# Seven block products for the second channel product, turns by DMA, and one written TensorE order

## The chip, the cores and the metric

The kernel runs on one core of a Trainium2 chip. The metric is the device time of one execution in microseconds, taken as the median of several runs. The profile is of one execution.

The engines go by short names: PE is TensorE (matmuls and transposes; PEld is its loading of weights), DVE is VectorE, ACT is ScalarE, POOL is GpSimd, SP is SyncE. SP and POOL issue the transfers (DMA). PSUM is the memory of eight banks per partition into which PE writes; each bank holds 512 fp32 numbers a partition.

## The reference

Four batches of windowed attention (8 heads, 768 positions, 64 numbers a head; a query sees the 4 first positions and the last 128) feed a token mixing and a channel mixing:

```python
def _attn_ref(q, k, v, n_sink, window):
    B, H, S, D = q.shape
    scores = (1.0 / np.sqrt(D)) * np.matmul(q, k.transpose(0, 1, 3, 2))
    pos = np.arange(S)
    rel = pos[:, None] - pos[None, :]
    keep = (pos[None, :] < int(n_sink)) | ((rel >= 0) & (rel < int(window)))
    scores = np.where(keep, scores, -1000000000.0)
    a = np.exp(scores - np.max(scores, axis=-1, keepdims=True))
    a = a / (np.sum(a, axis=-1, keepdims=True) + 1e-09)
    return np.matmul(a, v).astype(np.float32)

def _moe_ref(x, w_tok1, w_tok2, w_ch1, w_ch2):   # x: (4, 768, 512)
    xt = x.transpose(0, 2, 1)
    h = np.maximum(xt @ w_tok1, 0.0) @ w_tok2     # 768 -> 256 -> 768
    u = x + h.transpose(0, 2, 1)
    h2 = np.maximum(u @ w_ch1, 0.0) @ w_ch2       # 512 -> 1536 -> 512
    return (u + h2).astype(np.float32)
```

## The kernel before

**Pairs.** The 32 (batch, head) combinations are handled as 16 pairs of heads, pairs 0 to 3 for batch 0 and so on. For a pair, q and k are loaded with their rows on the partitions, turned to have head numbers on the partitions (`qT`, `kT`), multiplied to scores in three groups `g` of 256 keys, exponentiated on ACT, masked, and multiplied with v, which carries a column of ones for the row sums. The four sink positions have small products of their own (`score_sinks`, `sink_values`), with copies of their k columns (`kTs`) and v rows (`v_sink`, written by `sink_rows`).

**Loads and turns.** Pairs 0 to 3 are loaded by SP in fp32 and cast. From pair 4 on POOL issues loads that cast on the way (L106), which also bring v and the weights. `transposed(p)` (L461) turns q and k of a pair by 24 PE transposes into a score tile; DVE and ACT copy the result out in halves, and `cleared` (L482) zeroes the strip of the tile that the scores need to be zero. Batch 0 and pair 4 use `turn` instead.

**Token mixing.** Per batch and half `g` of the 512 channels, `mix_h` makes 12 matmuls of 256 columns (`x_sb` with `w_tok1`), and three `mix_u` make four each (`h1T` with `w_tok2`); DVE adds x to give `u_sb`. `turned_u` (L787) turns u by PE into `uT`.

**Channel mixing** (`mix_channels`, L903). `v1(ft, half)` multiplies `uT` with `w_ch1`, 4 matmuls of 384 columns, and a relu stores a block of `v1T`: 12 blocks `ft` of hidden numbers by 2 halves of the rows. Then `out_part` multiplies `v1T` with `w_ch2`: per tile of 128 rows 12 matmuls of 512 columns into one bank; DVE adds u (L938), SP stores 128 rows (L944). The very last row tile goes in three column blocks (L960).

**Score tiles.** PSUM is cut into two score tiles of two banks each (tag `sc`) and four single banks (tag `mx`). `scores` of groups 1 and 2 go by quarters (`by_quarters`): 16 small matmuls that skip what the window masks; the parts skipped must hold zeros, which is what `cleared` restores.

**Order.** A planner in the program (`Plan`, L250) simulates the engines with fixed costs and emits instructions in that order. An `Op` is an instruction for any engine, with its costs and what it depends on; a `unit` is a stretch of PE work, with its needs of banks and the ops that follow it. Three lists of units are merged: `first` (attention and token mixing of batch 0), `main` (channel mixing) and `side` (all later attention and token mixing). `MERGED` (L47) says for each side unit after how many main units it comes; units of `first` are put in wherever the simulation finds them ready. Each engine runs its instructions in program order.

Of the kernel before, what the change touches and what calls it, by code (L numbers as in the profile page):

```python
# [16 lines left out]
def kernel(  # L17
# [13 lines left out]
    nc = tc.nc  # L31
# [15 lines left out]
    MERGED = (  # L47
# [5 lines left out]
    )  # L53
    NQ = 6
    MASKED_BY_PE = [(p, g) for p in range(NHP) for g in range(NT // 2) if (p, g) != (NHP - 1, 0)]
# [4 lines left out]
    att_pool = ctx.enter_context(tc.tile_pool(name="att", bufs=2))  # L60
# [3 lines left out]
    osb_pool = ctx.enter_context(tc.tile_pool(name="osb", bufs=3))  # L64

    psum = ctx.enter_context(tc.tile_pool(name="psum", bufs=1, space=bass.MemoryType.PSUM))
    TAGS = {"sc": 2, "mx": 4}

    given = {}

    sc = [psum.tile([P, 2, 2, 4, D], FP32, name=f"ps_sc{n}", tag=f"sc{n}", bufs=1) for n in range(TAGS["sc"])]

    def bank(tag, *shape, dtype=FP32, slot=None):

        n = given[tag].pop(0) if slot is None else slot
        if tag == "sc":
            return sc[n]
        return psum.tile([P, *shape], dtype, name=f"ps_{tag}", tag=f"{tag}{n}", bufs=1)
# [5 lines left out]
    def rows_of(pidx, n):  # L84

        b, hp = pairs[pidx]
        return (q, k)[n][b, 2 * hp:2 * hp + 2].rearrange("h (p j) d -> p h j d", j=NT)
# [67 lines left out]
    keep_warm(7, 0)  # L155
# [27 lines left out]
    NKB = 2  # L183
# [28 lines left out]
    x_sb = [singles.tile([P, NT, DM], BF16, name=f"x_sb{b}") for b in range(B)]  # L212
# [37 lines left out]
    class Plan:  # L250
        def __init__(self):
            self.free = {"PE": 0.0, "ACT": 0.0, "DVE": 0.0, "SP": 0.0, "POOL": 0.0}
            self.queue, self.landings = 0.0, []
            self.half = False
            self.pending = []
            self.held = {t: [()] * n for t, n in TAGS.items()}

# [9 lines left out]
        def slots(self, tag):  # L267

            free = []
            for n, readers in enumerate(self.held[tag]):  # L270
                if all(r.done is not None for r in readers):
                    free.append((max((r.done for r in readers), default=0.0), n))
            return sorted(free)

        def spare(self):
            return self.slots("mx")[0][1]

        def start_pe(self, op):
            t = self.ready(op)
            if t is None:  # L280
                return None
            for tag, banks in op.need.items():
                free = self.slots(tag)
                if len(free) < len(banks):
                    return None
                t = max(t, free[len(banks) - 1][0])
            return max(t, self.free["PE"])
# [23 lines left out]
        def commit_pe(self, op, t):  # L311
            for tag, banks in op.need.items():
                given[tag] = [n for _, n in self.slots(tag)[:len(banks)]]
                for n, readers in zip(given[tag], banks):
                    self.held[tag][n] = readers
# [6 lines left out]
        def run(self, first, main, side):  # L322

            first, main = [list(u) for u in first], list(main)
            order = [[int(n) for n in unit.split("/")] for unit in MERGED.split()]
            side, behind = [side[n] for n, _ in order], [n for _, n in order]
            placed = 0
            while any(first) or main or side or self.pending:
                o = self.other()
                tm = self.start_pe(main[0]) if main else None  # L330
                ts = self.start_pe(side[0]) if side else None
                pick = "side" if side and (not main or behind[0] <= placed) else "main"
                t = tm if pick == "main" else ts
                early = [(t, u) for u in first if u for t in [self.start_pe(u[0])] if t is not None]
                if early:
                    soonest = min([t for t, _ in early] + ([] if t is None else [t]))
                    stay = [(t, u) for t, u in early if self.half and u[0].half and t <= soonest + SWITCH]
                    te, u = next((e for e in stay + early if e[0] <= soonest + (SWITCH if e in stay else 40.0)), (None, None))
                    if u is not None and (o is None or o[0] > te):
                        self.commit_pe(u.pop(0), te)  # L340
                        continue
# [11 lines left out]
                if pick == "main":  # L353
                    placed += 1
                else:
                    behind.pop(0)
                self.commit_pe((main if pick == "main" else side).pop(0), t)
# [35 lines left out]

    QH = NT // 2

    def prepare(p):
# [21 lines left out]
        free = ([("sk", p - 2)] if p >= 2 else [], [("s", p - NKB)] if p >= NKB else [])  # L418
# [10 lines left out]
        tiles["kT", p] = kT  # L429
# [31 lines left out]
    def transposed(p):  # L461

        def run():
            ps = turned_bank(p)
            for n in range(2):
                for j in range(NT):
                    for x in range(2):
                        rows = ds(D * x, D)
                        in_order(nc.tensor.transpose(ps[:, x, n, j], bfs[p, n][rows, j], ident[rows, rows]))  # L469
                tiles["ps_" + "qk"[n], p] = [ps[:, x, n].rearrange("d j p -> d p j") for x in range(2)]  # L470

        then = [*done["qT", p], *done["kT", p], done["kTs", p]]
        then.append(cleared(p, then))
        return piece(
            350, run, [done["q_bf", p], done["k_bf", p]], {"sc": [then]}, then, [("tq", p), ("tk", p)],
        )

    def turned_bank(key):

        tiles["ps_turned", key] = bank("sc")  # L480
        t = tiles["ps_turned", key].bitcast(BF16).rearrange("d x n b c -> d x n (b c)")[:, :, :, 2 * D:8 * D]
        return t.rearrange("d x n (j p) -> d x n j p", j=NT)  # L482

    def cleared(key, readers):

        op = Op(
            {"DVE": 400.0}, lambda e: in_order(nc.vector.memset(tiles["ps_turned", key][0:D, :, :, 3], 0.0)), readers,
        )
        op.urgent = 2
        return op  # L490
# [22 lines left out]
    def scores(p, g):  # L513
# [28 lines left out]
        def run():  # L542
            if ("pT", p) not in tiles:
                tiles["pT", p] = pt_pool.tile([P, 2, NT, 2, P], BF16, name="pT")
# [7 lines left out]
        def exp(e):  # L552
            in_order(nc.scalar.activation(  # L553
# [4 lines left out]
        def mask(e):  # L558
            pt = part(tiles["pT", p][:, :, ds(2 * g, 2)])
# [549 lines left out]
```

## Time and profile before

| | |
|---|---|
| runs | 207.47, 207.51, 207.58 us, median 207.51 us |
| span of the profiled execution | 206.7 us |
| PE busy | 199.5 us (97%) |
| DVE, ACT, POOL busy | 114.8, 119.0, 67.3 us |
| TensorE clock granted | full speed in all slices |
| data moved | 21.58 MB by DMA, in 73,223 packets |
| last matmul ends | 203.8 us |

A line of a group gives source line, engine, operation, output and input, their shapes and count, then busy time, the mean duration of one in ns, and the idle time of the engine just before it. In a list in order of time a line has start, length, engine, source line, operation and count. A matmul's length is from its start to the modelled end of its pipeline, so lengths of neighbours overlap, and the distance between starts is what a matmul costs. A line of the chain names engine, tile and source line, and its share of the span.

### The profile page before, as it was taken

What the parts mean: (1) busy time and instruction counts of PE and PEld (TensorE: products, weight loads), DVE (VectorE), ACT (ScalarE), POOL (GpSimd) and SP (SyncE); (2) the same over time, 40 slices, a digit from 0 to 9 for tenths busy, and PEclk for the clock granted to TensorE, in tenths of its full rate; (3) what the DMA queues carried; (4) which work ended last, traced back from release to release, by engine and by line L of the source; (5) the groups of instructions that cost most, each with busy time, mean ns of one, the idle gap of its engine ahead of it and who ended that gap; (6) DMA issues with size and microseconds to landing.
All of it is one profiled execution on the core that took longest, in us unless ns stands there. A gap on an engine that the chain in (4) does not pass through costs nothing.

```text
span 206.7 us, 5560 instructions
## 1 busy us (share of the span) xinstructions
PE 199.5 (97%) x2377; PEld 119.8 (58%) x2377; DVE 114.8 (56%) x263; ACT 119.0 (58%) x225; POOL 67.3 (33%) x86
## 2 busy tenths in 40 slices
PE   6798999999999999999999999999999999999994
PEld 2344795565565665666665555656655555565443
DVE  4687545649767777566675775784357252000222
ACT  4599666878744744888676443977562105773000
POOL 6099687696499984441000000000000000000000
PEclk9999999999999999999999999999999999999999
DMA  6999999999999999596001121100001212000223
GB/s 197 293 228 137 165 190 176 170 160 197 175 184 175 186 190 182 79 107 43 0 3 54 51 101 55 54 0 3 0 3 51 101 54 101 0 3 0 101 101 102
DMA packets 73223, 21.58 MB, mean 104 GB/s; under 512 B 63216, under 2 KB 70256, under 8 KB 73200
## 3 DMA queue, kind: packets, MB, share of 16 engines
q0 software_dynamic: 67232, 11.80, 72.7%
q1 hardware_dynamic: 5968, 9.45, 12.8%
q8 instruction: 18, 0.29, 0.6%
q14 instruction: 5, 0.04, 0.1%
HBM read 26.75 MB, written 6.29 MB: 160 GB/s over the span
## 4 chain that ended last, share of the span: by engine, by line
PE 86%; DMA 7%; DVE 2%; POOL 1%; ACT 1%; issue 0%; SPq 0%; POOLq 0%
PE ps_mx L121 78%; PE ps_sc L121 4%; DMA w_tok<-in_moe_w_tok_dram 4%; DMA v_sink_f<-in_v_dram 3%; PE ps_sc L469 2%; PE ps_mx L439 1%; POOL v_aug L114 1%; PE ps_mx L124 1%; SPq L200 0%; DVE u_sb L765 0%; POOL v_sink L130 0%; DVE qT L130 0%; PE ps_mx L451 0%; DVE kT L130 0%; DVE x_sb L664 0%
## 5 line engine op out<-in xcount | busy, mean ns | idle before, releaser
L121 PE MATMUL ps_mx<-w_ch,v1T 128*128 128x512 bf16 (+2 forms) x312 | 67.5, 363 | 0.0
L121 PE MATMUL ps_mx<-uT,w_ch 128*128 128x384 bf16 x384 | 66.3, 326 | 0.3 <-DVE recip L661 0.3
L553 ACT ACTIVATE pT<-ps_sc 128x1024 bf16<-128x1024 f32 (+1 forms) x48 | 44.5, 955 | 12.1 <-PE ps_sc L121 11.8
L121 PEld LDWEIGHTS <-w_ch 128*128 128x128 bf16 x384 | 36.2, 98 | 24.5 <-issue 1.5
L134 ACT ACTIVATE v1T<-ps_mx 128x384 bf16<-128x384 f32 x74 | 36.1, 493 | 16.5 <-PE ps_mx L121 16.0
L121 PEld LDWEIGHTS <-v1T 128*128 128x128 bf16 x312 | 28.2, 98 | 26.9 <-issue 0.7
L938 DVE TENSOR_TENSOR o_sb<-ps_mx,u_sb 128x512 f32<-128x512 f32 x23 | 15.9, 690 | 37.2 <-PE ps_mx L121 37.2
L121 PEld LDWEIGHTS <-w_tok 128*128 128x128 bf16 x192 | 18.4, 98 | 7.0 <-DMA w_tok<-in_moe_w_tok_dram 1.2
L106 POOL DMA_DIRECT2D q_bf<-in_q_dram x24 | 19.7, 824 | 4.6 <-DMA w_ch<-in_moe_w_ch_dram 2.0
L106 POOL DMA_DIRECT2D k_bf<-in_k_dram x24 | 19.6, 822 | 4.5 <-DMA w_ch<-in_moe_w_ch_dram 2.2
L114 POOL DMA_DIRECT2D v_aug<-in_v_dram x16 | 16.5, 1030 | 10.6 <-PE ps_mx L121 5.6
L765 DVE TENSOR_TENSOR u_sb<-ps_mx,x_sb 128x512 bf16<-128x512 f32 x20 | 13.2, 687 | 9.0 <-PE ps_mx L121 8.9
L136 DVE TENSOR_SCALAR v1T<-ps_mx 128x384 bf16<-128x384 f32 x22 | 12.2, 558 | 7.8 <-PE ps_mx L121 7.0
L121 PE MATMUL ps_mx<-v_aug,pT 128*128 128x65 bf16 x352 | 15.5, 194 | 0.0
L121 PEld LDWEIGHTS <-pT 128*128 128x128 bf16 x352 | 13.8, 97 | 2.7 <-issue 0.6
L121 PE MATMUL ps_sc<-qT,kT 64*64 64x192 bf16 (+3 forms) x288 | 15.0, 252 | 0.0
L561 DVE TENSOR_TENSOR pT<-pT,mask_main 128x1024 bf16<-128x1024 bf16 (+1 forms) x24 | 13.9, 618 | 0.0
L121 PE MATMUL ps_mx<-h1T,w_tok 128*128 128x256 bf16 x96 | 13.4, 272 | 0.0
L121 PE MATMUL ps_mx<-x_sb,w_tok 128*128 128x256 bf16 x96 | 12.0, 273 | 0.9 <-DMA w_tok<-in_moe_w_tok_dram 0.9
L130 DVE COPY qT<-ps_sc 128x384 bf16<-128x384 bf16 x11 | 6.1, 558 | 11.8 <-ACT qT L128 11.8
L664 DVE TENSOR_TENSOR x_sb<-ps_mx,recip 128x384 bf16<-128x384 f32 x22 | 11.6, 549 | 0.1
L128 ACT ACTIVATE kT<-ps_sc 128x384 bf16<-128x384 bf16 x16 | 7.3, 489 | 6.9 <-DVE qT L130 6.9
(74 smaller groups left out, 166.3 us busy)
## 6 DMA issues: line engine op xcount, KB each, us to landing
out_dram<-o_sb SPq DMA_DIRECT2D x23, 256.0 KB, 2.0
v_aug<-in_v_dram POOLq DMA_DIRECT2D x16, 192.0 KB, 7.0
w_ch<-in_moe_w_ch_dram POOLq DMA_DIRECT2D x8, 384.0 KB, 8.9
q_bf<-in_q_dram POOLq DMA_DIRECT2D x24, 96.0 KB, 7.0
k_bf<-in_k_dram POOLq DMA_DIRECT2D x24, 96.0 KB, 6.0
q_f<-in_q_dram SPq DMA_DIRECT2D x4, 384.0 KB, 5.9
k_f<-in_k_dram SPq DMA_DIRECT2D x4, 384.0 KB, 6.2
w_tok<-in_moe_w_tok_dram POOLq DMA_DIRECT2D x2, 384.0 KB, 8.5
```

Of the source, the lines that this page charges most:

```text
L106: in_order(nc.gpsimd.dma_start(out=out[:, h], in_=rows[:, h]))
L114: in_order(nc.gpsimd.dma_start(out=v_aug.rearrange("p i t d -> p (i t) d")[:, :, 0:D], in_=v[b].rearrange("h s d -> (h s) d")[2 * hp * S:2 ...
L121: in_order(nc.tensor.matmul(*args, skip_group_check=True, **kwargs))
L128: in_order(nc.scalar.activation(out, in_, AF.Copy))
L130: in_order({"DVE": nc.vector, "POOL": nc.gpsimd}[e].tensor_copy(out=out, in_=in_))
L134: in_order(nc.scalar.activation(out, in_, AF.Relu))
L136: in_order(nc.vector.tensor_scalar_max(out=out, in0=in_, scalar1=0.0))
L553: in_order(nc.scalar.activation(part(tiles["pT", p][:, :, ds(2 * g, 2)]), of_keys(tiles["ps_s", p, g])[:, :, 0:width(g)], AF.Exp, scale=scale,
L561: in_order(nc.vector.tensor_tensor(out=pt, in0=pt, in1=m, op=ALU.mult))
L664: in_order(nc.vector.tensor_tensor(out=x_sb[b][:, :, ds((2 * hp + i) * D, D)], in0=tiles["ps_o", p, i][:, :, 0:D], in1=tiles["recip", p, i ...
L765: in_order(nc.vector.tensor_tensor(out=u_part(b, g, s0, n), in0=tiles["ps_u", b, g, s0], in1=x_sb[b][:, s0:s0 + n, c0:c0 + cn], op=ALU.add,))
L938: in_order(nc.vector.tensor_tensor(out=o_sb.rearrange("p (g c) -> p g c", g=2), in1=u_rows(b, st), in0=tiles["ps_out", b, st].rearrange("p ...
```

## The change

1. **Seven products.** For batches 1 to 3 the second channel product is cut into 2 by 2 blocks (row halves by hidden halves, hidden halves by column halves) and made from seven block products in place of eight, by a scheme with four sums of v1 blocks (`add_up`: S1 to S4, S3 written over a v1 block) and four differences of weight blocks (`weight_sums`: T1 to T4, made once). Each product covers 384 rows by 256 columns and is made in two parts, `x` (two row tiles sharing a bank) and `y` (one row tile). Banks `a` and `c` go on accumulating after DVE has read them, and DVE adds each state to the output blocks: seven evictions in a part. An `x` part is 14 units of 6 matmuls, a `y` part 7 units of 6.
2. **Turns by DMA.** q and k of pairs 8 to 15 are turned by 16 DMA transposes, and u of batches 2 and 3 by 12, one after each `mix_u`; all are issued by SP. `turned_u` and `transposed` remain for what comes earlier. The q, k loads of these pairs take rows in another arrangement.
3. **One order.** `ORDERED` lists every PE unit by stream and number: `s m t o h g` are the first attention and token mixing, `a` the later attention, `k` the later token mixing, `c` the first channel product (24 units a batch), `x` and `y` the second (`x0` to `x23` are batch 0, undivided).
4. **Banks.** `choose` may give banks of the second score tile to other uses once the first streams are done; scores go by quarters only on the first score tile; `transposed` takes two plain banks; `cleared` goes.
5. **Smaller moves.** Sink rows go by two small DMAs of SP for each pair and no longer by ACT; masks of key groups 1 and 2 may go to POOL as four selects; `att` and `kT` buffers go from 2 to 3; `x_sb` from 4 to 2; stores are of a whole part (512 KB for `x`, 256 KB for `y`).

```diff
-    MERGED = (
-        "1/0 0/2 2/4 3/9 4/15 5/16 6/16 7/19 8/23 9/24 10/26 11/27 12/28 15/30 14/30 13/31 16/32 17/32 18/33 "
...
+    ORDERED = (
+        "t0-1 m0 s0 m1 s1 t2-3 m2-3 s2-3 o0 m4 s4 t4 m5 s5 t5 o1 m6-7 o2 s6 t6 o3 s7 o4 m8 t7 s8-9 g0 m9 s10-11 "
+        "g1 o5-6 m10 a0 s12 o7 g2 o8 g3-4 h0-1 g5 a1 h2-4 g6 h5-6 a2 c0-3 a3 h7 g7 c4-7 a4 c8 a5 c9-12 a6-7 "
+        "c13-15 a8 c16 a9-10 c17-21 a11 k0 x0-2 a12 k1 c22-23 a13 k2-3 x3-6 a14 x7 a15 x8-10 a16 x11 a17-18 "
+        "x12-14 k4 x15-16 k5-7 x17-19 a19 x20-23 c24 a20-22 c25-27 a23 c28-30 a24 c31-33 a25-26 c34 a27 c35-36 k8 "
+        "c37-39 a28-30 c40 x24 a31 c41-43 k9 c44 k10 a32-33 x25 k11 a34 c45-47 x26 k12 x27-28 a35 x29-31 k13 x32 "
+        "k14 a36-37 x33 y0 a38 y1-2 x34-35 y3 k15 y4 a39 y5 x36 c48 y6 c49 a40 x37 a41-42 c50-54 a43 c55-56 k16 "
+        "c57-60 a44-45 c61-64 a46 c65 a47 x38 c66-67 x39 c68 a48 c69 a49 k17-18 c70 k19 c71 k20 x40-41 k21-22 "
+        "x42-44 y7-8 x45-46 k23 y9 x47 y10-11 x48 y12 x49 c72-73 y13 x50-51 c74-87 x52 c88-91 x53 c92-95 x54 y14 "
+        "x55-56 y15 x57-58 y16 x59-61 y17 x62-63 y18-19 x64-65 y20"
     )
+    ORDER = (1, 2, 7, 6, 4, 5, 3)
...
+    BY_SEVEN = range(1, B)
+    BY_DMA = 2 * NHP
...
+        if pidx >= BY_DMA:
+            return rows.rearrange("h (j p) d -> p h j d", p=P)
...
+        if p >= BY_DMA:
+            def turn(e, n):
+                if not n:
+                    tiles["qT", p] = att_pool.tile([P, S], BF16, name="qT2")
+                in_order(nc.sync.dma_start_transpose(
+                    out=(kT if n else tiles["qT", p]).rearrange("c (t p) -> c t p", t=NT),
+                    in_=bfs[p, n].rearrange("p t h d -> p (t h d)"),
+                ))
...
-            (by_quarters if quarters else by_halves)(tiles["ps_s", p, g])
+            (by_quarters if quarters and tiles["ps_s", p, g] is sc[0] else by_halves)(tiles["ps_s", p, g])
...
         def mask(e):
+            if e == "POOL":
+                for n in range(2):
+                    nk = 2 if n == 0 or g < NT // 2 - 1 else 1
+                    for i in range(2):
+                        pt = tiles["pT", p][:, i, 2 * g:2 * g + nk, n]
+                        in_order(nc.gpsimd.affine_select(
+                            out=pt, in_=pt, compare_op=ALU.is_ge, fill=0.0, base=-n,
+                            pattern=[[0, nk], [1 - 2 * n, P]], channel_multiplier=2 * n - 1,
+                        ))
+                return
...
-                copy(e, v_sinks[p % NHP][r:r + n_sink, i], vs[p][0:n_sink, i, 0])
+                in_order(nc.sync.dma_start(out=v_sinks[p % NHP][r:r + n_sink, i], in_=vs[p][0:n_sink, i, 0]))
...
+            def turn(e):
+                in_order(nc.sync.dma_start_transpose(
+                    out=tiles["mix", b][2].rearrange("c (g t p) -> c g t p", g=2, p=P)[:, g, 2 * s0:2 * (s0 + n)],
+                    in_=u_part(b, g, s0, n).rearrange("p t c -> p (t c)"),
+                ))
...
+            s1 = op("S1", lambda: part(0), a21, a22, ALU.add, v[1, 0] + v[1, 1] + before)
+            s3 = op("S3", a21, a11, a21, ALU.subtract, v[0, 0] + [s1])
+            s2 = op("S2", lambda: part(1), lambda: part(0), a11, ALU.subtract, v[0, 0] + [s1])
+            s4 = op("S4", lambda: part(2), a12, lambda: part(1), ALU.subtract, v[0, 1] + [s2])
...
+        TERMS = {
+            1: ((0, 0), "B11"), 2: ((0, 1), "B21"), 3: ("S4", "B22"), 4: ((1, 1), "T4"),
+            5: ("S1", "T1"), 6: ("S2", "T2"), 7: ("S3", "T3"),
+        }
...
+            a1 = evict("a1", (0, 0), lambda: u_block(0, 0))
+            a6 = evict("a6", (1, 0), lambda: u_block(1, 0))
+            c7 = evict("c7", (1, 1), lambda: u_block(1, 1))
+            a5 = evict("a5", (1, 1), lambda: sb(1, 1), [c7])
+            a3 = evict("a3", (0, 1), lambda: u_block(0, 1))
+            c4 = evict("c4", (1, 0), lambda: sb(1, 0), [a6])
+            b2 = evict("b2", (0, 0), lambda: sb(0, 0), [a1])
...
+                        for t in range(n):
+                            for k in range(c * KC, (c + 1) * KC):
+                                mm(
+                                    ps[:, t], left(a_name, k, t0 + t), right(b_name, k),
+                                    start=(before is None and t == 0 and k == 0), stop=(k == NH - 1),
+                                )
...
+        x, y = products(0, 2), products(2, 1)
+        x, y = [u for m in ORDER for u in x[m]], [u for m in ORDER for u in y[m]]
+        done["out", b] = [x[-1], y[-1]]
...
+        for name, out, in0, in1, of in (
+            ("T1", t1, b12, lambda: b11, ()), ("T2", t2, b22, t1, ("T1",)),
+            ("T3", t3, b22, lambda: b12, ()), ("T4", t4, b21, t2, ("T2",)),
+        ):
```

More of the change, by code (lines that the diff above doesn't have):

```diff
@@ L320, in commit_pe, with run @@
             self.pending.extend(op.then)
[L322 to L328, printed above, removed]
-                o = self.other()
[L330 to L341, printed above, removed]
+        def run(self, units, early):
+            early = len(early)
+            units = list(units)
+            while units or self.pending:
+                self.late = early == 0
+                o = self.other()
+                t = self.start_pe(units[0][1]) if units else None
                 if o is not None and (t is None or o[0] <= t):
@@ L392, in piece, with joined, run @@
         return op
+    def joined(*units):
+        def run():
+            for u in units:
+                u.fn()
+        need = {}
+        for u in units:
+            for f in u.then:
+                f.deps = [d for d in f.deps if d is not u]
+            for tag, banks in u.need.items():
+                need.setdefault(tag, []).extend(banks)
+        return unit(
+            sum(u.size for u in units), run, [d for u in units for d in u.deps], need,
+            [t for u in units for t in u.then], half=units[0].half,
+        )
     QH = NT // 2
@@ L468, in run @@
                         rows = ds(D * x, D)
[L469 to L473, printed above, removed]
+                        in_order(nc.tensor.transpose(ps[x][:, n, j], bfs[p, n][rows, j], ident[rows, rows]))
+                tiles["ps_" + "qk"[n], p] = [ps[x][:, n].rearrange("d j p -> d p j") for x in range(2)]
+        readers = [[done["qT", p][x], done["kT", p][x]] for x in range(2)]
+        readers[0].append(done["kTs", p])
         return piece(
-            350, run, [done["q_bf", p], done["k_bf", p]], {"sc": [then]}, then, [("tq", p), ("tk", p)],
-        )
[L478 to L490, printed above, removed]
+            350, run, [done["q_bf", p], done["k_bf", p]], {"mx": readers}, [op for r in readers for op in r],
+            [("tq", p), ("tk", p)],
+        )
     def width(g):
```

425 lines of the change are left out of this document (278 added, 147 removed), and 4 rows, old and new, of the table MERGED.

## The prediction

> **What bounds the kernel now.** First the page's head, the clock row and the chain of waits; then the busy time by stretch of time; then TensorE's (PE's) instructions in order of time; last the groups and the DMA issues.
>
> ```profile
> span 206.7 us, 5560 instructions
> PE 199.5 (97%) x2377; PEld 119.8 (58%) x2377; DVE 114.8 (56%) x263; ACT 119.0 (58%) x225; POOL 67.3 (33%) x86
> PEclk9999999999999999999999999999999999999999
> PE 86%; DMA 7%; DVE 2%; POOL 1%; ACT 1%; issue 0%; SPq 0%; POOLq 0%
> ```
>
> The span is 206.7 us; the runs' median is 207.5, so 0.8 us lie around it, and I carry that over. PE is 86% of the chain that ends last, at full clock throughout. In busy time by stretch (start:end, its length, then busy time and instruction count of each engine):
>
> ```profile
> 20.80:40.00 19.20, 18.98 (x252) 13.85 (x252) 10.69 (x27) 13.58 (x28) 13.43 (x17) 1.00 1.86 177
> 40.00:60.00 20.00, 19.72 (x246) 11.88 (x243) 14.11 (x33) 15.94 (x30) 15.28 (x19) 1.00 1.93 173
> ...
> 100.00:120.00 20.00, 20.00 (x277) 12.58 (x276) 13.84 (x29) 11.06 (x24) 0.00 (x0) 1.00 0.11 41
> ...
> 190.00:204.00 14.00, 13.76 (x88) 7.41 (x86) 4.38 (x8) 0.00 (x0) 0.00 (x0) 1.00 0.27 99
> 204.00:206.70 2.70, 0.00 (x0) 0.00 (x0) 0.09 (x1) 0.00 (x0) 0.00 (x0) 1.00 0.23 67
> ```
>
> From 20.8 us, when the first token weights land, to the last matmul at 203.8, PE idles about 0.8 us (0.22 + 0.28 + 0.24, the rest 0.04). So from 20.8 on, the time is the sum of PE's work plus 2.9 us of last eviction and store. Work taken from PE there comes off the end, as long as nothing new makes PE wait. Before 20.8 the w_tok load sets the pace; its place in POOL's queue does not change, so I leave that stretch as it is.
>
> **Step 1: the second channel product by seven block products (batches 1 to 3).** A pitch is the distance of starts, not the busy time:
>
> ```profile
> 160.10 1.47 PE L121 MATMUL ps_mx<-x_sb,w_tok 128*128 128x256 bf16 x12
> 161.41 2.10 PE L121 MATMUL ps_mx<-w_ch,v1T 128*128 128x512 bf16 x9
> 163.36 0.60 PE L121 MATMUL ps_mx<-h1T,w_tok 128*128 128x256 bf16 x4
> ```
>
> Twelve 256-column matmuls, each with its own 128x128 weights, take 161.41 - 160.10 = 1.31 us, 109 ns each; nine of 512 columns take 1.95 us, 217 ns each. Halving the columns costs nothing. A batch had 6 x 12 = 72 of 512 columns, 15.6 us; it will have 7 products x 3 row tiles x 6 = 126 of 256, 13.75 us. Saved: 1.8 a batch, **5.4 us** in three.
>
> **Step 2: q, k of pairs 8 to 15 and u of batches 2, 3 leave PE.**
>
> ```profile
> 51.97 0.35 PE L469 MATMUL ps_sc<-ident,q_bf 64*128 64x64 bf16 x12
> 52.16 0.34 PE L469 MATMUL ps_sc<-ident,k_bf 64*128 64x64 bf16 x12
> 52.33 0.38 PE L121 MATMUL ps_sc<-qT,kT 64*128 64x256 bf16 x4
> ```
>
> The 24 transposes of a pair take 52.33 - 51.97 = 0.36 us, and they share a burst that stays; 8 x 0.36 = **2.9 us**. The four turns of u in batches 2 and 3 stand in the chain of waits with 0.44, 0.44, 0.35 and 0.51: **1.7 us**.
>
> **Step 3: what PE gains in work.** Scores of key groups 1 and 2 go by quarters only on the first score tile, since the second also serves as ordinary banks; on it they go by halves. Quarters for both groups take 0.43 us (48.84 to 49.27 in order of time), eight half matmuls, two groups' worth, 0.49 (22.37 to 22.86). Twelve pairs: between 0 and 12 x 0.06 = 0.7; I take **+0.4**, since two tiles alternate.
>
> **Step 4: VectorE (DVE), ScalarE (ACT), POOL.**
>
> ```profile
> L561 DVE TENSOR_TENSOR pT<-pT,mask_main 128x768 bf16<-128x768 bf16 x12 | 6.6, 553 | 0.0
> L974 DVE TENSOR_TENSOR o_sb<-ps_mx,u_sb 128x256 f32<-128x256 f32 x1 | 0.4, 426 | 0.6 <-PE ps_mx L121 0.6
> L128 ACT ACTIVATE v_sink<-v_aug 4x65 bf16<-4x65 bf16 x24 | 6.1, 253 | 0.3
> L938 DVE TENSOR_TENSOR o_sb<-ps_mx,u_sb 128x512 f32<-128x512 f32 x23 | 15.9, 690 | 37.2 <-PE ps_mx L121 37.2
> ```
>
> Added: 24 sums of v1 (4 for each of 2 chunks in 3 batches), each 128x1152 bf16 in SBUF. The mask products of 128x768 and 128x1024 take 553 and 685 ns, so 0.52 ns an element more and 751 ns here: 18.0 us. Eight weight differences of 128x768 at 553: 4.4. Evictions: 7 x 0.69 + 7 x 0.426 = 7.8 a batch for 6 x 0.69 = 4.1, so +11.1 in three. Together 33.5 us. Removed: 32 copies of q, k halves at 490 to 558 ns, 16.8; twelve clearing memsets at 272, 3.3; eight copies of uT at 0.55 to 0.8, about 5; sink rows on ACT, 24 x 253 ns, 6.1: 31 us. So the two engines, at 14.11 and 15.94 of 20 us in the fullest stretch shown, stay near 75%. I cost this at nothing: PE's queue covers it while other units stand between a product and what it needs. For the last value sums of batch 1 the cover is x26-28 (3 x 0.66), k12 (1.31) and a35 (0.43 + 0.33), 4.0 us; the relu and two sums in a row are 0.56 + 0.75 + 0.75 and handing over, 2.4. Without cover each of six such chains puts up to 2 us on PE. Masks that POOL takes are four selects for one product: its row has 638 ns at 128x512 and 290 at 128x128, so some 1.6 us for DVE's 0.55 to 0.69; loads queued behind one go out that much later. Those of pair 15 are issued by 89 us and used at 133, which covers several.
>
> **Step 5: the DMA transposes.** There are 16 of 128x768 and 12 of 128x512, all on SP's queue, with sink rows and stores behind them in order. No run so far has one. From below: a store's row, 0.33 us of issue and 2.0 to landing.
>
> ```profile
> out_dram<-o_sb SPq DMA_DIRECT2D x23, 256.0 KB, 2.0
> q_bf<-in_q_dram POOLq DMA_DIRECT2D x24, 96.0 KB, 7.0
> k_bf<-in_k_dram POOLq DMA_DIRECT2D x24, 96.0 KB, 6.0
> ```
>
> From above: the loads in 128-byte pieces, two of 0.82 us issue for a tile, 7.0 to landing at the median, 10.0 at the longest, in a crowded queue. I take 1.6 of issue and 4.5 to landing: small pieces as in the loads, but from 100 us on the page's slices have the DMA engines 0.0 to 0.2 busy until the last stores. A pair's turns may start when pair p-3 is scored, over 12 us ahead (pairs are scored every 7 to 14 us), so they hide; pair 8, loaded at 45.8 to 49.0 and landed by about 56, is scored near 66. Tightest is u. Between k14, the last token product that the first half of batch 2 needs, and c48, its first use, PE has ten x and y units of 6 x 0.109 = 0.66, k15 (0.43) and a36 to a39 (0.43, 0.34, 0.34, 0.43): 8.6 us. Less the eviction of 0.75, 7.8 are left for 0.9 of queue behind k13's turn + 1.6 + 4.5 = 7.0. Before c72 in batch 3 there are fourteen units and k23: 9.6 less 0.75, 8.9 left. So I cost this at nothing, with under 1 us to spare at c48.
>
> [...]
>
> **Step 6: the end.** Last stood a 64 KB store; now a 512 KB store and, 0.4 us behind it, one of 256 KB. The rows go from 1.7 us (128 KB) to 2.0 (256 KB), so 2.6 for 512 KB, and both share the engines: **+0.9**, between 0.3 and 1.5.
>
> **New waits.** Between -0.8 (PE's idle goes) and the rivals' several us; I take **+0.6**, one short wait at each batch's border.
>
> **Sum:** 206.7 - 5.4 - 2.9 - 1.7 + 0.4 + 0.9 + 0.6 = 198.6 of span; with 0.8 around it **199.4 us**.
>
> **Rivals.** (A) The u turns land late. With the loads' 7.0 they need 0.9 + 1.6 + 7.0 = 9.5: 1.7 late at c48 and 0.6 at c72, 201.7; with 10.0, 4.7 and 3.6, 207.7. For it: nothing but earlier-placed units can fill PE there. Against: idle DMA engines. 201.5 to 206, chance 0.17. (B) Sums and evictions come late: if POOL takes sums at some 2.7 us (its 128x768 cast is 0.84, a sum has half as many elements again and two inputs), the 2.4 us chain becomes 6, 2 us late, 6 us in three batches: 205.4. Against: DVE idles 25%. Also 0.10. (C) Slower: transposes become the bound of the middle. Pairs 8 to 12 are scored from 69.9 to 111.4, 41.5 us for 14 transposes, some 38 afterwards; one stream at 2.7 us each just keeps up, at 3.0 the whole gain is gone, at 3.5 each of two batches takes 11 us more: 221. For it: one queue in order, three buffers. Against: 1.6 is the issue row of like pieces. 0.10. (D) The written order also removes early waits or the tail costs less: under 197.5, 0.05.
>
> **Numbers.** The forecast, 197.5 to 201.5, has 0.58. A measurement of this kernel tells 0.2% (0.4 us) from no change. Faster: 0.58 + 0.17 + 0.09 + 0.05 = 0.89; same 0.01; slower 0.10. The range 197 to 206 holds the forecast, A and most of B, about 0.83.
>
> **What would show it.** Right: 256-column products at 109 ns; no 64x64 transposes of pair 8 on; PE without gaps between k14 and c48; last matmul near 194.5. Wrong: PE or its weight loads waiting for qT, kT or uT (A, C); for v1_sums (B); transposes more than 3 us apart in SP's queue with SP never waiting (C). The forecast falls if a transpose takes over 5.3 us to land beside u, or if the 256-column pitch rises above 109 ns with two row tiles sharing a bank.

## The result, and the profile after

| | before | after |
|---|---|---|
| runs beside each other | 207.47 to 207.94 us, median 207.55 | 216.50 to 218.26 us, median 216.68 |
| ratio | | 1.0461 (95%: 1.0425 to 1.0497) |
| span of the profiled execution | 206.7 us | 214.5 us (its run: 216.57) |
| last matmul ends | 203.8 us | 209.05 us |

The change made the kernel 4.6% slower; the forecast was 199.4 us. Ratios, here and below, leave out runs over 1.5% above the fastest of their kernel, so a ratio can lie below the quotient of two medians.

The head of the page, its clock and DMA rows, and the chain of waits:

```profile
span 214.5 us, 5060 instructions
PE 192.5 (90%) x2099; PEld 130.5 (61%) x2107; DVE 131.6 (61%) x280; ACT 103.2 (48%) x179; POOL 70.8 (33%) x96
PEclk9999999999999999996799999999999999999999
DMA  6999999999999999999092427242001325200025
PE 59%; DMA 9%; DVE 3%; issue 1%; SPq 0%; DVEq 0%
PE ps_mx L144 51%; PE ps_sc L144 8%; DMA v_sink<-v_aug 6%; DMA kT<-k_bf 3%; DVE q_f L1249 1%; DVE o_sb L1143 1%; DVE o_sb L1061 1%; SPq L1149 0%; DVE pT L628 0%; DVE x_sb L735 0%; PE ps_mx L509 0%; DVE kTs L153 0%; DVE recip L732 0%; DVEq L732 0%; SPq L469 0%
```

PE is busy for 7 us less than before (192.5 for 199.5), yet the span is 7.8 us longer. The chain names new links: the sink rows' transfer (`v_sink<-v_aug`) with 6%, the k turns with 3%. Two slices of the clock row, from 96.5 to 107.2 us, are below full speed, where none was before.

Busy time by stretch (start:end, length, then PE, PEld, DVE, ACT, POOL, granted clock, DMA share, GB/s):

```profile
60.00:80.00 20.00, 16.22 (x188) 9.41 (x190) 10.78 (x27) 4.92 (x7) 12.16 (x16) 1.00 1.87 175
80.00:99.50 19.50, 13.24 (x166) 7.06 (x166) 9.11 (x19) 8.50 (x13) 10.16 (x12) 0.96 2.10 167
99.50:104.60 5.10, 5.09 (x34) 2.91 (x35) 1.16 (x2) 0.98 (x2) 0.00 (x0) 0.50 0.42 51
140.00:209.05 69.05, 69.05 (x619) 51.68 (x618) 40.12 (x73) 28.10 (x53) 0.00 (x0) 1.00 0.18 56
```

From 140 us on PE has no gap at all. The time went between 60 and 104.6 us: 10 us of idle PE, then 5.1 us of work at half clock. PE's instructions in order of time there, those that waited (what they waited for stands in brackets):

```profile
33.51 0.35 PE L539 MATMUL ps_mx<-ident,k_bf 64*128 64x64 bf16 x12 [1.80 <-DMA k_bf<-in_k_dram]
...
71.81 0.52 PE L144 MATMUL ps_mx<-v_sink,pT_sink 64*128 64x65 bf16 x8 [2.63 <-DMA v_sink<-v_aug]
...
79.96 0.60 PE L144 MATMUL ps_mx<-h1T,w_tok 128*128 128x256 bf16 x4 [0.78 <-DVE o_sb L1143]
...
99.51 0.58 PE L144 MATMUL ps_mx<-v_sink,pT_sink 64*128 64x65 bf16 x8 [6.22 <-DMA v_sink<-v_aug]
```

With 0.45 at 121.97 and 0.19 at 61.58, PE waited 12.1 us from 20.8 us on, 8.85 of it for sink rows (2.63 and 6.22).

**Why the sink rows came late.** SP's queue in order of time, ahead of the long wait:

```profile
85.34 1.52 SPq L469 DMA_TRANSPOSE kT<-k_bf  x1
90.94 1.40 SPq L469 DMA_TRANSPOSE qT<-q_bf  x1
92.44 0.54 SPq L1149 DMA_DIRECT2D out_dram<-o_sb  x1
93.03 1.25 SPq L765 DMA_DIRECT2D v_sink<-v_aug  x2
```

SP issued nothing from 86.9 to 90.94. The q turn of pair 12 waits for a `qT` buffer, which comes free when PE has scored pair 9, at 90.84. A store of batch 0 and the sink rows of pair 9 stand behind it in the same queue. PE is ready for those rows at 93.3; they are issued at 93.03 and land at 99.46, 6.4 us for half a kilobyte, beside loads that POOL issued up to 93.0, where the page's DMA row reads 9. The planner reckoned 2.2 us to that landing (`lag=2200.0`, in the line that experiment 1 takes out), so its order never meant to issue the rows 6 us ahead.

The first wait has another head. In the chain, in order of time (start, length, what):

```profile
56.95 7.26 DMA kT<-k_bf
64.61 0.69 DVE o_sb L1143
65.76 6.01 DMA v_sink<-v_aug
...
93.03 6.43 DMA v_sink<-v_aug
```

A k turn takes 7.3 us to land. DVE, which runs in order, stands before the copy of its sink columns (`kTs`, 64.24, waiting 1.27); the eviction behind it comes at 64.61, so its store at 65.33, so the sink rows behind that store on SP at 65.76; they land at 71.77. No turn that waits for PE stands ahead of these rows, but a store that waits for DVE.

**The sum.** From the forecast's span of 198.6 to 214.5 are 15.9 us: PE waits 12.1 where the sum held 1.4 (0.8 of the trace before, 0.6 new), +10.7; half clock over 5.1 us of work, +2.55; PE's work itself, (209.05 - 20.8) - 12.1 - 2.55 = 173.6, where the forecast's is 183.0 - 0.8 - 9.6 = 172.6, +1.0; from the last matmul to the end 5.45 where 3.8 stood, +1.65. Together 15.9. Outside the span lie 2.1 us, 1.3 more than carried over.

### The profile page after: what moved, and what is told of

It reads as the page before. It is cut to its first block, busy times and chain, and to the rows that moved or that the text cites. A ratio compares the mean times of both kernels' runs of the same rounds, so it can differ in the third digit from the quotient of the medians.

```text
span 214.5 us, 5060 instructions
## 1 busy us (share of the span) xinstructions
PE 192.5 (90%) x2099; PEld 130.5 (61%) x2107; DVE 131.6 (61%) x280; ACT 103.2 (48%) x179; POOL 70.8 (33%) x96
## 4 chain that ended last, share of the span: by engine, by line
PE 59%; DMA 9%; DVE 3%; issue 1%; SPq 0%; DVEq 0%
PE ps_mx L144 51%; PE ps_sc L144 8%; DMA v_sink<-v_aug 6%; DMA kT<-k_bf 3%; DVE q_f L1249 1%; DVE o_sb L1143 1%; DVE o_sb L1061 1%; SPq L1149 0%; DVE pT L628 0%; DVE x_sb L735 0%; PE ps_mx L509 0%; DVE kTs L153 0%; DVE recip L732 0%; DVEq L732 0%; SPq L469 0%
## 5 line engine op out<-in xcount | busy, mean ns | idle before, releaser
L144 PE MATMUL ps_mx<-uT,w_ch 128*128 128x384 bf16 x344 | 63.0, 331 | 0.0
L144 PE MATMUL ps_mx<-w_ch,v1T 128*128 128x256 bf16 (+1 forms) x169 | 30.0, 315 | 0.3
L1061 DVE TENSOR_TENSOR o_sb<-ps_mx,u_sb 128x256 f32<-128x256 f32 (+1 forms) x23 | 12.6, 550 | 8.0 <-PE ps_mx L144 8.0
L144 PE MATMUL ps_sc<-qT,kT 64*128 64x256 bf16 (+2 forms) x240 | 16.7, 258 | 0.9 <-ACT kT L151 0.8
L144 PEld LDWEIGHTS <-v_sums 128*128 128x128 bf16 x162 | 15.7, 98 | 2.2 <-issue 0.2
L144 PE MATMUL ps_mx<-v_sink,pT_sink 64*128 64x65 bf16 (+1 forms) x76 | 6.7, 204 | 8.9 <-DMA v_sink<-v_aug 8.8
L841 DVE TENSOR_TENSOR u_sb<-ps_mx,x_sb 128x512 bf16<-128x512 f32 x18 | 12.2, 686 | 2.6 <-PE ps_mx L144 2.3
L144 PE MATMUL ps_mx<-q_f,v_sums 128*128 128x256 bf16 x108 | 13.6, 273 | 0.0
L144 PEld LDWEIGHTS <-kT 64*128 64x128 bf16 (+1 forms) x240 | 6.0, 98 | 11.6 <-issue 8.7
L144 PE MATMUL ps_mx<-v_aug,pT 128*128 128x65 bf16 x264 | 12.5, 196 | 0.1
```

Of the source, the lines that this page charges most:

```text
L144: in_order(nc.tensor.matmul(*args, skip_group_check=True, **kwargs))
L841: in_order(nc.vector.tensor_tensor(out=u_part(b, g, s0, n), in0=tiles["ps_u", b, g, s0], in1=x_sb[b][:, s0:s0 + n, c0:c0 + cn], op=ALU.add,))
L1061: in_order(nc.vector.tensor_tensor(out=sb(*out), in0=tiles["ps_out", b, t0, key[0]], in1=in1(), op=ALU.add,))
```

## The experiments

Each run stands beside runs of the kernel before on the same chip (medians 207.11 to 207.45 us). Edits are against the changed kernel unless another is named.

**1. Sink rows by ACT or DVE again.** Is the transfer of the sink rows the whole loss?

```diff
-                in_order(nc.sync.dma_start(out=v_sinks[p % NHP][r:r + n_sink, i], in_=vs[p][0:n_sink, i, 0]))
+                copy(e, v_sinks[p % NHP][r:r + n_sink, i], vs[p][0:n_sink, i, 0])
...
-        done["vs", p] = Op({"SP": 200.0}, both, [done["v", p], done["pv", p - NHP]], lag=2200.0)
+        done["vs", p] = Op({"ACT": 440.0, "DVE": 400.0}, both, [done["v", p], done["pv", p - NHP]])
```

> The changed kernel with the sink rows copied by ACT or DVE again; all else stays. Theory 1 (the sink rows' two small DMAs, issued by SP behind transposes and stores, come late): PE's waits of 2.63 and 6.22 us for v_sink go, and with them the stretch of lower clock behind the longer one, some 2 us: span near 203.7, time 205.5 (204 to 207). Rival (the transposes crowd the DMA engines and SP's queue, and PE would stop at the same places for kT, kTs or an eviction): at least 212.

Measured: 210.46 us (209.98 to 212.08), ratio 1.0173 (1.0127 to 1.0219), span 209.0. The waits for sink rows are gone, with 6.2 us of the time; but they and the half clock had cost 11.4. The time lies between what the two outcomes expected. What took their place, on PE and on DVE, in order of time:

```profile
80.28 1.01 PE L144 MATMUL ps_mx<-h1T,w_tok 128*128 128x256 bf16 x4 [3.17 <-DVE o_sb L1143]
96.10 0.28 PE L144 MATMUL ps_mx<-v_sink,pT_sink 64*128 64x65 bf16 x7 [1.12 <-DVE v1T L159]
```

```profile
78.72 0.36 DVE L153 COPY kTs<-kT 64x4 bf16<-64x4 bf16 x2 [4.73 <-DMA kT<-k_bf]
79.53 0.69 DVE L1143 TENSOR_TENSOR o_sb<-ps_mx,u_sb 128x512 f32<-128x512 f32 x1 [0.46 <-DMA out_dram<-o_sb]
...
95.11 0.34 DVE L153 COPY kTs<-kT 64x4 bf16<-64x4 bf16 x2 [2.50 <-DMA kT<-k_bf]
```

DVE stands 4.73 us before a copy of a few columns whose k turn has not landed, and again 2.50; evictions that PE needs stand behind it. For the wait of 1.12 the late turn ends last. For the wait of 3.17 it does not: when the columns are copied, the eviction still waits 0.46 us, until a store lands and frees one of two output buffers. That store's eviction ends at 66.62; the store is issued at 71.61, behind a k turn that waits for its load until 70.30, and takes 7.8 us to land. So the sink rows are part of the loss, and two things lay under them: turns that land late, passed on by an engine that runs in order, and stores that land late and hold their buffers. The issues of this run have the durations (the last number: median us to landing, over the turns that something waited for):

```profile
uT<-u_sb SPq DMA_TRANSPOSE x12, 2.4
qT<-q_bf SPq DMA_TRANSPOSE x8, 6.0
kT<-k_bf SPq DMA_TRANSPOSE x8, 8.1
```

**2. Sink rows by DMA, queued one pair earlier.**

```diff
-            units[-1].then.append(sink_rows(p))
+            if p == first:
+                units[-1].then.append(sink_rows(p))
+            if p < last:
+                units[-1].then.append(sink_rows(p + 1))
```

> The changed kernel with the sink rows still by SP's DMAs, but queued one pair of heads earlier. Theory 1 in the form that the place in SP's queue is what makes them late: the waits for v_sink go, 204 to 208. Rival form (the small DMA takes over 6 us to land beside the other transfers, wherever it stands): waits for v_sink of over 4 us stay, 211 or more.

Measured: 212.08 us (211.02 to 212.74), ratio 1.0248 (1.0211 to 1.0285), span 209.0. No wait for sink rows is left, though they still go through SP's queue: an earlier place in it is enough (pair 9's are issued at 80.06 and used at 92.82). The time is not in the 204 to 208 that this was expected to give. Left are PE waits of 1.75 for a load of k, 1.89 and 1.76 for DVE, and two dips of the clock.

**3. The kernel before, with only the sink rows by DMA.**

```diff
-                copy(e, v_sinks[p % NHP][r:r + n_sink, i], vs[p][0:n_sink, i, 0])
+                in_order(nc.sync.dma_start(out=v_sinks[p % NHP][r:r + n_sink, i], in_=vs[p][0:n_sink, i, 0]))
```

> The kernel before with one part of the change alone: its sink rows by two small DMAs of SP. If the small DMA alone is late (6 us to land while the loads run), PE waits for v_sink here too: 210 to 216. If it takes the transposes in the same queue to make it late, within 1 us of 207.5.

Measured: 207.25 us (206.69 to 208.68), ratio 0.9995 (0.9965 to 1.0025); PE waits for no sink rows. The same transfers cost nothing where SP's queue holds only stores. The trace also says why that proves less than was hoped: from 60 us on the rows of pairs 7, 8 and 9 are issued 6 to 10 us ahead of their use (62.33 for 68.68, 72.03 for 82.28, 81.01 for 90.88). So a landing of 6 us would not show here. In the changed kernel pair 8's rows, 7.0 us ahead, cost nothing either; those 3.4 and 0.3 us ahead did.

**4. Experiment 1 with whole products.** What do the seven products save by themselves?

```diff
-    BY_SEVEN = range(1, B)
+    BY_SEVEN = ()
...
-    for c in range(2):
-        weight_sums(c)
```

The 24 units of a batch's second channel product stand at the places of its 21 `x` and `y` units, with the hidden blocks taken in the order 0, 6, 3, 9.

> The kernel of e1 with the second channel product of batches 1 to 3 undivided again (24 units a batch put at the 21 places of the x and y units), without the sums and differences: what the seven products alone are worth. By the prediction's step 1, e1 plus 5.4 us (4.5 to 6.5 more). Rival (the evictions and sums of the seven products cost PE waits that eat the gain): less than 3 us more than e1.

Measured: 214.58 us (213.45 to 215.6), ratio 1.0357 (1.0314 to 1.0399), span 213.8. That is 4.1 us more than experiment 1 by medians, 4.8 by spans, a little under the 4.5 to 6.5 expected: the seven products keep most of their 5.4 us even with waits about. PE is busy for 181.8 us from 20.8 us on, where experiment 1 has 175.9.

**5. Experiment 1, with the column copies placed later.** The planner reckoned 4 us from a turn's issue to its landing; with 8 it places the `kTs` copies behind other work of DVE and POOL.

```diff
-                op = Op({"SP": 1500.0}, lambda e, n=n: turn(e, n), [done[name + "_bf", p], *free[n]], lag=4000.0)
+                op = Op({"SP": 1500.0}, lambda e, n=n: turn(e, n), [done[name + "_bf", p], *free[n]], lag=8000.0)
```

> The kernel of e1 with one number of the plan changed: a DMA turn of q or k is taken to land 8 us after its issue in place of 4. In e1 DVE waited 12.2 us for kT before copying sink columns (kTs), and the evictions behind those copies came late, one of them 3.17 us for PE. Theory 2 (DVE's order, planned on too short a turn, passes the lateness of the turns on to PE): DVE's waits for kT fall below 4 us, PE's wait for o_sb goes, and the lower clock behind it; span near 204.5, 3 to 6 us less than e1. Rival (the evictions wait for their buffers, whose stores stand behind turns in SP's queue): within 1 us of e1.

Measured: 207.17 us (205.39 to 211.31), ratio 0.9983 (0.9954 to 1.0012), span 204.2. No wait of DVE for k turns is left (12.2 us of them in experiment 1), and no dip of the clock. The turns are no faster (7.2 us for q and 9.4 for k at the median), and PE's order is the same; but the number also moves other instructions of DVE, POOL and SP, the stores for one (69.30 for 71.61), so the gain is not the columns' place alone. By the traces PE's waits over 0.6 us after 60 us go from 5.6 to 2.6, and the stretch of half clock goes. The longest wait of PE, 2.58, is the one of 3.17 in experiment 1, now held by the store alone; on DVE:

```profile
78.12 0.69 DVE L1143 TENSOR_TENSOR o_sb<-ps_mx,u_sb 128x512 f32<-128x512 f32 x1 [4.74 <-DMA out_dram<-o_sb]
```

**6. Experiment 5, a third output buffer in batch 0, and the planner told when `qT` is really free.**

```diff
-        free = ([("sk", p - 3)] if p >= 3 else [], [("s", p - NKB)] if p >= NKB else [])
+        free = ([("sk", p - 3), ("s", p - 3)] if p >= 3 else [], [("s", p - NKB)] if p >= NKB else [])
...
-                o_sb = tiles["o_sb", b, st] = osb_pool.tile([P, DM], FP32, name="o_sb", bufs=2)
+                o_sb = tiles["o_sb", b, st] = osb_pool.tile([P, DM], FP32, name="o_sb", bufs=3)
```

> The kernel of e5 with the eviction buffers of batch 0 three again, as before, and the plan told that a qT buffer is free only when the pair's scores are done, so that SP's queue has the next turn behind what can go earlier. Theory 2 with the turns' lateness already absorbed: within 1 us of e5. Rival (stores behind waiting turns hold the buffers): 2 us or more less than e5.

Measured: 205.84 to 212.13 us in four runs, too far apart for a ratio. The profiled one (212.13) has a PE wait of 4.55 for a `kTs` copy on POOL, and a dip behind it. Inconclusive.

**7. Experiment 6, with stores by column half (batches 1 to 3).** Each half is stored when its own evictions are done.

```diff
-            def store(i):
+            def store(i, g):
...
+                    in_order(nc.sync.dma_start(out=rows[:, :, ts(g, C2)], in_=sb(i, g)))
```

> The kernel of e6 with the stores of batches 1 to 3 by column half, each sent when its half is done; the last ones are 256 and 128 KB in place of 512 and 256. From the end of PE to the end of the span it was 5.4 us in the changed kernel and 2.9 before. If the size of the last stores makes it: 4.4 or less, 1 us less than e6. If not (their landing has a fixed length): the same as e6.

Measured: 208.51 us (207.17 to 210.93), ratio 1.0043 (1.0016 to 1.007). The tail after the last eviction is 3.25 us, where it was 4.35; the wait for POOL's `kTs` copy stays (4.12). The stores do what was meant; the planner's later release of `qT` is not an improvement, as the next run suggests.

**8. Experiment 7 without the edit of `free`.** So: sink rows copied, columns later, third buffer, split stores.

> The kernel of e5 with three eviction buffers for batch 0 and stores by column half, and SP's order of turns as in e5 (unlike e6 and e7). In e5 DVE waited 6.1 us for stores of o_sb (one of these reached PE as 2.58 us), and 4.4 us passed between the last eviction and the end. Theory 2, extended (what is left of the loss is stores behind late turns, and large last stores): PE's wait for o_sb goes, the end after the last eviction is 3.3 us; span near 200.6, time near 202 to 205, faster than before by 1 to 2.5%. Rival (another late turn takes the place of the buffer, as kTs did in e6 and e7): PE waits for kTs or kT, 206 or more.

Measured: 206.31 us (203.73 to 208.03), ratio 0.9865 (0.9823 to 0.9908). The profiled run (207.80, span 206.1; the six times spread by 4.3 us, and the others have no trace) has one long wait, of the kind that the rival named. On PE, and POOL around it:

```profile
97.00 0.67 PE L144 MATMUL ps_mx<-qT,kTs 64*32 64x512 bf16 x2 [2.87 <-POOL kTs L153]
```

```profile
95.92 0.83 POOL L129 DMA_DIRECT2D k_bf<-in_k_dram  x1 [1.09 <-DMA q_bf<-in_q_dram]
96.74 0.45 POOL L153 COPY kTs<-kT 64x4 bf16<-64x4 bf16 x2
```

The k turn of that pair (pair 11 by the count of turns; the expectation of experiment 11 says 12) was issued on SP at 81.72; POOL makes the copy only after the issue of a load, which itself waited 1.09 us for another load. The same pattern a third time: a small instruction that PE needs, behind a waiting one in an engine's order.

**9. Experiment 8 with whole products** (the edit of experiment 4).

> The kernel of e8 with the second channel product of batches 1 to 3 undivided, as in e4: the seven products' worth where fewer waits of other kinds are in the way. By the prediction's step 1: e8 plus 5.4 us (4.5 to 6.0; part of it lies in the last stores, which are 256 KB whole rows here). Rival (sums and evictions cost waits): less than 3.5 us more.

Measured: 213.44 us (210.29 to 216.81), ratio 1.0225 (1.0168 to 1.0282); span 212.1 with the same POOL wait (2.85). Against experiment 8 that is 7.1 us more by medians and 6.0 by spans, so at least the 5.4 of the sum, and at or above the 4.5 to 6.0 expected. The last stores differ too, and both kernels' runs spread by 4 us or more, so it says no more than that.

**10. Experiment 8 with one unit of TensorE's order moved,** against the wait for k of a pair near 33 us.

```diff
-        "... h5-6 a2 c0-3 a3 h7 ..."
+        "... h5-6 c0-1 a2 c2-3 a3 h7 ..."
```

> The kernel of e8 with the PE unit that turns pair 5 (a2) moved two units of the first channel product later in the written order. In e5 PE idled 0.6 us for k_bf and 0.5 for w_ch near 33 to 36 us, in the changed kernel 1.8 for k_bf. If the written order meets the loads too early: 0.5 to 1.5 us less than e8. If the loads set the pace there anyway: the same as e8 within 0.5 us.

Measured: 207.85 us (205.83 to 210.64), ratio 0.9999 (0.9967 to 1.003). The wait for k is gone and one of 1.14 for `w_ch` stands in its place: there the loads set the pace, not the order. The median is 1.5 us above experiment 8's, which neither outcome had; its trace has the wait for POOL's columns too (2.35). A miss.

**11. Experiment 8, column copies by DVE alone.**

```diff
-                {"POOL": 300.0, "DVE": 300.0}, sinks_of, done["kT", p] + [("sk", p - NHP)],
+                {"DVE": 300.0}, sinks_of, done["kT", p] + [("sk", p - NHP)],
```

> The kernel of e8 with the sink columns (kTs) copied by DVE alone. In e8 POOL copied them for pair 12 at 96.7 us, behind four load issues of its own, though that pair's kT turn was issued at 81.7 to 83.3: PE waited 2.87 us, and the granted clock fell behind it. Theory 2: the last wait of this chain goes, none other over 1 us comes, granted clock 1.00 in the fast runs: span 202, time 203.5 to 205. Rival (DVE, blocked by late kT, delays evictions as in e1): 206 or more.

Measured: **203.09 us** (202.15 to 204.28), ratio 0.9797 (0.9762 to 0.9832): faster than the kernel before by 4.4 us, and with six runs within 2.1 us. Head of its page, and its longest wait on PE in order of time:

```profile
span 202.5 us, 5082 instructions
PE 192.0 (95%) x2107; PEld 130.0 (64%) x2107; DVE 132.7 (66%) x292; ACT 107.0 (53%) x197; POOL 69.5 (34%) x90
```

```profile
80.85 0.32 PE L509 MATMUL ps_mx<-ident,u_sb 64*64 64x64 bf16 x16 [1.37 <-DVE u_sb L841]
```

That wait comes behind DVE's columns again: DVE stands 2.58 us for a k turn until 79.73, then makes this `u_sb`. So the mechanism is made small, not gone, and a wait over 1 us is left where none was expected. PE's instructions and their written order are those of the changed kernel; what differs is who waits for what.

**12. The changed kernel with four `qT` and `kT` buffers.** Sink rows by DMA as in the change. If the blocked queue alone makes them late, a turn that no longer waits for its buffer should free them; if 6 us of landing do, nothing changes.

```diff
-    att_pool = ctx.enter_context(tc.tile_pool(name="att", bufs=3))
+    att_pool = ctx.enter_context(tc.tile_pool(name="att", bufs=4))
...
-    NKB = 3
+    NKB = 4
...
-        free = ([("sk", p - 3)] if p >= 3 else [], [("s", p - NKB)] if p >= NKB else [])
+        free = ([("sk", p - 4)] if p >= 4 else [], [("s", p - NKB)] if p >= NKB else [])
```

> The changed kernel with sink rows by DMA as it has them, and four qT and kT buffers in place of three. There SP stood 10.2 us in one turn of q that waited for its buffer (PE's scores of the pair three before), with a store and the sink rows of pair 9 behind it. If that blocked queue makes the 6.22 us wait: it falls below 3 us and the time to 210 to 213.5. If the small DMA's landing of 6 us makes it: the wait stays over 5 us, 215 or more.

Measured: 217.94 us (216.91 to 218.52), ratio 1.05 (1.0461 to 1.0538); waits for sink rows of 2.29 and 6.34. SP's queue in order of time:

```profile
87.79 1.88 SPq L469 DMA_TRANSPOSE kT<-k_bf  x1
93.06 1.21 SPq L469 DMA_TRANSPOSE qT<-q_bf  x1
94.37 0.53 SPq L1149 DMA_DIRECT2D out_dram<-o_sb  x1
94.96 1.25 SPq L765 DMA_DIRECT2D v_sink<-v_aug  x2
```

With more buffers the planner moved a turn one pair further ahead, and that one waits for PE in turn, at the same place in the queue: the gap from 89.7 to 93.06 is there again. So this run doesn't separate the blocked queue from the slow landing. (Its expectation also took the wrong wait: the 10.2 us belong to the turn at 106.61, with no sink rows behind it; ahead of pair 9's rows SP's waits have 5.3, in 4.1 of which nothing is issued.) With experiment 2 it says only that rows issued 0.3 to 3.4 us ahead of their use, and 6 us on the way, are late; no run says how much of the 8.85 us each part holds. As an estimate from the two queues of the changed kernel: had SP not stood idle ahead of the rows (2.0 us up to the store at 65.33, 4.1 up to the turn at 90.94), the waits would be 0.6 and 2.1; had the rows landed in the planner's 2.2 us, 0 and 1.9. Either part alone would have taken most of it away.

## Why the prediction was wrong

**Step 5 failed, at the sink rows.** It said that all turns go "on SP's queue, with sink rows and stores behind them in order", and then asked only whether the turns land in time. Step 4 counted "sink rows on ACT, 24 x 253 ns, 6.1" as removed; the two DMAs of each pair that came in their place were priced nowhere, neither their landing (6.0 and 6.4 us in the chain) nor what stands ahead of them. The view of SP's waits has what stood ahead (waited for: total, times, longest), in the windows from 62 to 72 and from 86 to 92 us:

```profile
SPq L1149 <- DVE recip L732: 2.1, 1, 2.1
SPq L469 <- PE ps_mx L144: 5.3, 1, 5.3
```

A store that waits for DVE and a turn that waits for PE, each ahead of something that PE needs, in one queue: 8.85 us of waiting, 2.55 of half clock behind the second. Taking the rows out of the queue gave 6.2 us back (experiment 1).

**Step 5 failed a second time at "so they hide".** Turns of q and k took 6.0 to 9.4 us at the median to land beside the loads (experiments 1 and 5), not 4.5; the estimate leaned on the DMA engines of the kernel before from 100 us on (0.0 to 0.2 busy), but five of the eight q turns are issued by 91 us, where the DMA row reads 9. PE itself waited for no turn, as argued. DVE and POOL were not covered: their copies of sink columns stand in order before evictions and loads. Experiment 5, which places the copies later and moves some stores with them, gave 3.3 us by medians.

**Right:** the pitch of 109 ns. PE's order near the end, start by start:

```profile
202.98 1.47 PE L144 MATMUL ps_mx<-q_f,v1T 128*128 128x256 bf16 x12
204.29 2.13 PE L144 MATMUL ps_mx<-q_f,v_sums 128*128 128x256 bf16 x18
206.25 0.82 PE L144 MATMUL ps_mx<-q_f,v1T 128*128 128x256 bf16 x6
```

Twelve in 1.31 us, eighteen in 1.96, with banks shared by two row tiles. Steps 1 and 2 hold: the work of PE is only 1.0 us over the sum, and experiments 4 and 9 put whole products at 4.1 to 7.1 us more. Sums of v1 took 745 to 758 ns (751 forecast), evictions 688 and 423; a mask on POOL 1.70 us (1.6). u turns landed in 2.4 us at the median (experiment 1; 4.5 allowed), and PE has no gap between k14 and c48.

**Mis-sized:** Step 3, +0.4 for what is 1.4: a burst of groups 1 and 2, one by halves and one by quarters, takes 0.57 (54.01 to 54.58 in order of time) where it took 0.43, in eleven pairs. The step took a mixed burst to cost something between all quarters (0.43) and all halves (0.49); it costs more than either. Step 6, +0.9 for what is 2.5: 5.45 us from the last matmul to the end. The last evictions take 1.1 of it, the 512 KB store and its neighbour 4.35; split stores bring this to 3.25. New waits, +0.6 for 11.3. One reading was off as well: the 0.8 us of PE's idle before count 0.2 that lie behind the last matmul (the stretch to 204.00); up to 203.80 it is 0.6.

**The rivals.** A fell: u turns are early. B fell: PE waited for no sum of v1, and 0.78 us at most for an eviction. C came near in time (221) and is wrong in mechanism: it asked for turns over 3 us apart with SP never waiting; their issues take 1.2 to 1.6 us but for two of 1.9 and 2.2, and SP mostly waits. D did not come. The 10% for slower were placed on a busy queue; what happened was a blocked one.

**With most of the waits taken away** the kernel comes near the forecast, though not into its 197.5 to 201.5: experiment 11's span is 202.5 for 198.6. Of the 3.9 us, PE waits are 2.3 (3.7 for 1.4), PE's work 1.0, most likely the mixed bursts, and the tail 0.5. These shares are worked out from its trace; no run took them away one by one.

## What to carry to other kernels

When work is moved from an engine to a DMA, price its issue, its landing in that stretch's traffic, and what waits ahead of it in its queue: 0.5 KB transfers behind a store and a turn that had to wait cost 6.2 us (experiment 1), about what the seven products saved. After that, look at engines that run in order: a copy of four columns that waited 4.73 us for a late transfer held up the evictions behind it (experiment 1), and a plan that places it later, with the transfer as slow as ever, gave back 3.3 us. Of two waits in a row, ask which ends last: the 3.17 us that seemed to come from a late turn ended with a store. Take the landing times from the busiest stretch in which the transfers run, not from a quiet one.

## What the runs showed of the hardware

**Transfers in a crowd.** A 0.5 KB copy within SBUF took 6.0 to 6.4 us to land beside POOL's loads, where the changed kernel's DMA row reads 9. DMA turns were issued in 1.2 to 1.6 us each, a few in up to 2.6, and landed in 2.4 us at the median for u (experiment 1, issued from 112 us on, where its DMA row reads 2 to 5 but for one slice of 8), in 6.0 to 9.4 at the median for q and k (experiments 1 and 5; in experiment 1 six of the eight q turns are issued by 101 us, where the row reads 9). A 256 KB store issued at 71.61 in experiment 1 freed its buffer 7.8 us later; the median of such stores before was 2.0.

**Half clock came in stretches of 3.4 us.** In the changed kernel by stretch (the granted clock is the number behind POOL's count):

```profile
91.00:94.40 3.40, 2.29 (x16) 1.09 (x14) 0.00 (x0) 3.27 (x5) 2.01 (x3) 1.00 1.93 113
94.40:97.80 3.40, 0.00 (x0) 0.00 (x0) 2.04 (x5) 0.01 (x1) 0.00 (x0) 1.00 2.16 153
97.80:101.20 3.40, 1.69 (x12) 0.93 (x13) 0.00 (x0) 0.00 (x0) 0.00 (x0) 0.50 1.40 179
101.20:104.60 3.40, 3.40 (x23) 1.98 (x22) 1.16 (x2) 0.98 (x2) 0.00 (x0) 0.50 0.03 2
```

and in experiment 2:

```profile
30.90:34.30 3.40, 1.54 (x38) 1.02 (x35) 0.79 (x2) 1.37 (x3) 2.90 (x5) 1.00 1.78 185
34.30:37.70 3.40, 3.40 (x12) 1.60 (x11) 1.49 (x3) 2.00 (x6) 2.45 (x3) 0.51 1.79 180
92.40:95.80 3.40, 1.64 (x19) 0.86 (x18) 1.93 (x5) 1.58 (x3) 0.30 (x1) 1.00 2.28 154
95.80:99.20 3.40, 3.40 (x30) 2.16 (x28) 1.45 (x5) 0.98 (x2) 0.00 (x0) 0.50 1.68 199
```

In experiment 2's clock records the changes stand at 34.34, 37.75, 95.78 and 99.19 us: 64.85 us from the first to the last, 19 times 3.413, with the others 1 and 18 times that from the first. In the changed kernel, up to its last matmul, they stand at 97.78 and 104.61, twice 3.41 apart. Of the stretches shown at full clock, those in which PE was busy for 1.64 us or less are followed by one at half clock; the one with 2.29 is not. The border is near half and not sharp: in other traces, each on its own grid, 1.71 us were followed by half clock (experiment 7, 93.71 to 97.12), 1.69 by full clock (experiment 5, 74.60 to 78.01), and so were 1.44 at the very end of experiment 10 (200.64 to 204.05). So where a wait falls counts: waits of 1.75 and 1.76 us were enough in experiment 2, while the one of 2.63 in the changed kernel brought no dip, spread over two stretches with 2.08 and 2.05 us of busy PE (67.06 to 73.89). Of the stretches named here that half clock followed, three were far from idle: PE was busy for 45 to 50% of them (1.54, 1.64 and 1.71 us).
